# Casting loads on GpSimd's queue and crossbar transposes of q and k, in a kernel of sliding-window attention and a two-layer MLP

## Chip, core and metric

One core of a Trainium2 chip runs the kernel. The metric is the device time of one launch in microseconds (us). Five engines work side by side, each with a queue of its own: TensorE (PE; matmuls and transposes, its weight loads shown as PEld), VectorE (DVE), ScalarE (ACT), GpSimd (POOL) and SyncE (SP), which here only issues DMAs. DMAs are issued from a queue of an engine and carried out by sixteen DMA engines.

## The reference

```python
def _attn_ref(q, k, v):                      # each (8, 8, 576, 64), float32
    B, H, S, D = q.shape
    window = 128
    scores = np.matmul(q, k.transpose(0, 1, 3, 2)) / np.sqrt(D)
    rel = pos[:, None] - pos[None, :]
    slopes = 2.0 ** (-8.0 * (np.arange(H) + 1) / H)
    bias = slopes[:, None, None] * (-np.abs(rel))[None, :, :]
    mask = (rel >= 0) & (rel < window)
    scores = np.where(mask, scores + bias[None], -1e9)
    attn = softmax(scores)
    return np.matmul(attn, v)

def _moe_ref(x, w_in, w_out):                # x (4608, 512), w_in (512, 2048), w_out (2048, 512)
    h = x @ w_in
    g = h * np.clip(h + 3.0, 0.0, 6.0) / 6.0
    return g @ w_out
```

The attention output, with its heads side by side, is the `x` of the second part. A query sees itself and the 127 keys before it, so a block of 128 queries needs two blocks of 128 keys: its own (the diagonal block, lower triangle) and the one before (the off block, strictly upper triangle).

## The kernel before

**Attention.** The work goes by pair groups `g`: batch `b = g // 4` and a pair `hp = g % 4` of heads, 32 groups in all. A batch of 576 tokens is five blocks of tokens, the last of 64. For every group, `transposes` (L151) turns q and k by ten 128x128 TensorE transposes into `qT` and `kT`, through a PSUM tile `tp` that DVE copies out (L158). `scores_diag` (L161) multiplies the diagonal blocks of both heads into a PSUM tile `sc`, ACT takes the exponential (L173, with scale and position bias), and POOL cuts the triangle with an affine select (L176). `scores_off` (L181) does the same for the off blocks and for the last, 64-wide diagonal block (`p4`): L199, L202, and on POOL L204 and L207. `values` (L212) multiplies with v, to which a column of ones is appended, so that column 64 of `av` is the sum for the softmax; DVE takes its reciprocal (L230) and scales (L231). It is called twice, for blocks 0 to 2 and 3 to 4, with one `av` buffer. `back` (L235) transposes the result on TensorE and DVE copies it (L242) into `xT`, which keeps all 4,608 tokens.

**MLP.** It runs over nine tiles of 512 tokens in units of four matmuls of 512 columns. An up unit (`moe_up`, L248) makes one 128-row block of the hidden layer in a PSUM tile `hps` (two buffers); ACT makes a Relu of it (L257) and DVE the product (L258). A down unit (`moe_down`, L261) is a quarter of one 128-token output block; after the fourth, ACT or DVE copies the block to `osb` (L272, L274) and SP stores it (L275). A tile has 16 up and 16 down units; all are put in one list, and the down units of a tile go between the up units of the next. `fill(n)` (L286) puts the next n units of the list into TensorE's order, but an up unit only if the attention of every batch that its tokens come from is complete (`done`).

**Order.** The order of TensorE is written out by hand (L313 to L337): an iteration g does the scores of group g, the values and the back transposes of group g-1, the transposes of group g+1, and eight units of the list in between. The order on the other engines is left to the framework's scheduler. After the last iteration `fill` places what is left of the list.

**Loads.** q, k and v are loaded as float32 by SP's queue (`load_pair` for batch 0, `load_all`, L89, for the others: 15 DMAs per batch, each in pieces of 256 bytes, one head of one token) into four buffers, and cast to bfloat16: batch 0 by DVE (L132 to L137), the others by POOL (L142 to L147). Both weight matrices are loaded by POOL's queue, cast on the way, in four DMAs each (L119, L125).

PSUM has eight banks: `sc` two (one buffer), `av` one, `tp` two, `hps` two, `ops` (the down output) one.

Of the kernel before, what the change touches and what calls it, by code (L numbers as in the profile page):

```python
# [10 lines left out]
FP32 = mybir.dt.float32  # L11
# [7 lines left out]
def kernel(  # L19
# [20 lines left out]
    W = D + 1  # L40
    slopes = [2.0 ** (-8.0 * (h + 1) / H) for h in range(H)]
# [3 lines left out]
    n_nt = Ntok // NT  # L45

# [5 lines left out]
    bias3 = perm.tile([128, 1], FP32)  # L52
    rel_i = perm.tile([128, 1], INT32)
# [4 lines left out]
    loads = ctx.enter_context(tc.tile_pool(name="loads", bufs=4))  # L58
    held = ctx.enter_context(tc.tile_pool(name="held", bufs=1))
    qkt = ctx.enter_context(tc.tile_pool(name="qkt", bufs=3))  # L60
    ppool = ctx.enter_context(tc.tile_pool(name="ppool", bufs=3))
    small = ctx.enter_context(tc.tile_pool(name="small", bufs=4))
# [3 lines left out]
    ps_sc = ctx.enter_context(tc.tile_pool(name="ps_sc", bufs=1, space=bass.MemoryType.PSUM))  # L66
    ps_av = ctx.enter_context(tc.tile_pool(name="ps_av", bufs=1, space=bass.MemoryType.PSUM))
    ps_tp = ctx.enter_context(tc.tile_pool(name="ps_tp", bufs=2, space=bass.MemoryType.PSUM))
# [3 lines left out]
    qbuf = [held.tile([128, NQ, H * D], BF16, name=f"qbuf{i}") for i in range(2)]  # L72
    kbuf = [held.tile([128, NQ, H * D], BF16, name=f"kbuf{i}") for i in range(2)]
    vbuf = [held.tile([128, NQ, H, W], BF16, name=f"vbuf{i}") for i in range(2)]
    p4buf = [held.tile([128, 2, 128], BF16, name=f"p4buf{i}") for i in range(2)]

    srcs = (("qf", q), ("kf", k), ("vf", v))

    def new_loads():
        return {nm: loads.tile([128, NQ, H, D], FP32, tag="ld", name=nm) for nm, _ in srcs}  # L80

    def load_pair(got, b, hp):
        for nm, src in srcs:
            for h in (2 * hp, 2 * hp + 1):
                nc.sync.dma_start(out=got[nm][:, 0:4, h, :],
                                  in_=src[b, h, 0:512, :].rearrange("(t p) d -> p t d", p=128))
                nc.sync.dma_start(out=got[nm][:LAST, 4, h, :], in_=src[b, h, 512:S, :])  # L87

    def load_all(got, b):  # L89
        for nm, src in srcs:  # L90
            for j in range(NQ):
                n = min(128, S - j * 128)
                nc.sync.dma_start(
                    out=got[nm][:n, j, :, :],
                    in_=src[b, :, ds(j * 128, n), :].rearrange("h p d -> p h d"))

    got0 = new_loads()
    for hp in range(NP):
        load_pair(got0, 0, hp)

    make_identity(nc, ident)
    nc.vector.memset(bias3, 0.5)
    nc.gpsimd.iota(rel_i, pattern=[[0, 1]], base=0, channel_multiplier=1)
    nc.vector.tensor_copy(out=rel_f, in_=rel_i)
    for h in range(H):
        nc.vector.tensor_scalar(out=bias_d[:, h:h + 1], in0=rel_f, scalar1=-64.0,
                                scalar2=slopes[h], op0=ALU.add, op1=ALU.mult)
        nc.vector.tensor_scalar(out=bias_o[:, h:h + 1], in0=rel_f, scalar1=-192.0,
                                scalar2=slopes[h], op0=ALU.add, op1=ALU.mult)
    for i in range(2):  # L110
        nc.vector.memset(vbuf[i][:, :, :, D:W], 1.0)
        nc.vector.memset(vbuf[i][64:128, 4, :, 0:D], 0.0)
        nc.vector.memset(qbuf[i][64:128, 4, :], 0.0)
        nc.vector.memset(kbuf[i][64:128, 4, :], 0.0)
        nc.vector.memset(p4buf[i], 1.0)
# [13 lines left out]
    def cast_pair(got, b, hp, eng):  # L129
        for nm, dst in (("qf", qbuf[b % 2]), ("kf", kbuf[b % 2])):  # L130
            s = got[nm].rearrange("p j h d -> p j (h d)")
            eng.tensor_copy(out=dst[:, 0:4, ts(hp, 128)], in_=s[:, 0:4, ts(hp, 128)])  # L132
            eng.tensor_copy(out=dst[:LAST, 4, ts(hp, 128)], in_=s[:LAST, 4, ts(hp, 128)])
        hs = slice(2 * hp, 2 * hp + 2)
        vb = vbuf[b % 2]
        eng.tensor_copy(out=vb[:, 0:4, hs, 0:D], in_=got["vf"][:, 0:4, hs, :])
        eng.tensor_copy(out=vb[:LAST, 4, hs, 0:D], in_=got["vf"][:LAST, 4, hs, :])  # L137

    def cast_all(got, b):
        for nm, dst in (("qf", qbuf[b % 2]), ("kf", kbuf[b % 2])):  # L140
            s = got[nm].rearrange("p j h d -> p j (h d)")
            nc.gpsimd.tensor_copy(out=dst[:, 0:4, :], in_=s[:, 0:4, :])  # L142
            nc.gpsimd.tensor_copy(out=dst[:LAST, 4, :], in_=s[:LAST, 4, :])
        vb = vbuf[b % 2]
        nc.gpsimd.tensor_copy(out=vb[:, 0:4, :, 0:D].rearrange("p j h d -> p (j h) d"),
                              in_=got["vf"][:, 0:4, :, :].rearrange("p j h d -> p (j h) d"))
        nc.gpsimd.tensor_copy(out=vb[:LAST, 4, :, 0:D], in_=got["vf"][:LAST, 4, :, :])  # L147

    st = {}

    def transposes(g):  # L151
        b, hp = divmod(g, NP)
        for src, nm in ((qbuf[b % 2], "qT"), (kbuf[b % 2], "kT")):
            tp = ps_tp.tile([128, SP], BF16, tag="tp", name="tp")
            for j in range(NQ):
                nc.tensor.transpose(tp[:, ts(j, 128)], src[:, j, ts(hp, 128)], ident)  # L156
            t = qkt.tile([128, SP], BF16, tag=nm, name=nm)
            nc.vector.tensor_copy(out=t, in_=tp)  # L158
            st[g, nm] = t

    def scores_diag(g):  # L161
        b, hp = divmod(g, NP)
        qT, kT = st[g, "qT"], st[g, "kT"]
        sc = ps_sc.tile([128, 2, 512], FP32, tag="sc", name="sc")
        for j in range(4):
            for e in range(2):
                r = slice(e * D, (e + 1) * D)
                nc.tensor.matmul(sc[:, e, ts(j, 128)], lhsT=kT[r, ts(j, 128)],  # L168
                                 rhs=qT[r, ts(j, 128)], start=True, stop=True)
        pd = ppool.tile([128, 2, 4, 128], BF16, tag="pd", name="pd")  # L170
        for e in range(2):
            h = 2 * hp + e
            nc.scalar.activation(out=pd[:, e, :, :].rearrange("p j c -> p (j c)"),  # L173
                                 in_=sc[:, e, :], func=ACT.Exp,
                                 bias=bias_d[:, h:h + 1], scale=scale)
            nc.gpsimd.affine_select(out=pd[:, e, :, :], in_=pd[:, e, :, :],  # L176
                                    pattern=[[0, 4], [1, 128]], channel_multiplier=-1, base=0,
                                    compare_op=ALU.is_ge, fill=0.0)
        st[g, "pd"] = pd

    def scores_off(g):  # L181
        b, hp = divmod(g, NP)
        qT, kT = st[g, "qT"], st[g, "kT"]
        sc = ps_sc.tile([128, 2, 512], FP32, tag="sc", name="sc")
        for j in range(4):
            n = 128 if j < 3 else LAST
            for e in range(2):
                r = slice(e * D, (e + 1) * D)
                nc.tensor.matmul(sc[:, e, ds(j * 128, n)], lhsT=kT[r, ts(j, 128)],  # L189
                                 rhs=qT[r, ds((j + 1) * 128, n)], start=True, stop=True)  # L190
        for e in range(2):
            r = slice(e * D, (e + 1) * D)
            nc.tensor.matmul(sc[:, e, 448:512], lhsT=kT[r, 512:640],  # L193
                             rhs=qT[r, 512:576], start=True, stop=True)
        po = ppool.tile([128, 2, 4, 128], BF16, tag="po", name="po")
        p4 = p4buf[g % 2]
        for e in range(2):
            h = 2 * hp + e
            nc.scalar.activation(out=po[:, e, :, :].rearrange("p j c -> p (j c)"),  # L199
                                 in_=sc[:, e, :], func=ACT.Exp,  # L200
                                 bias=bias_o[:, h:h + 1], scale=scale)
            nc.scalar.activation(out=p4[:, e, 0:64], in_=sc[:, e, 448:512], func=ACT.Exp,  # L202
                                 bias=bias_d[:, h:h + 1], scale=scale)
            nc.gpsimd.affine_select(out=po[:, e, :, :], in_=po[:, e, :, :],  # L204
                                    pattern=[[0, 4], [-1, 128]], channel_multiplier=1, base=-1,
                                    compare_op=ALU.is_ge, fill=0.0)
        nc.gpsimd.affine_select(out=p4[:, :, 0:64], in_=p4[:, :, 0:64],  # L207
                                pattern=[[0, 2], [1, 64]], channel_multiplier=-1, base=0,
                                compare_op=ALU.is_ge, fill=0.0)
        st[g, "po"] = po  # L210
# [157 lines left out]
```

The softmax here doesn't subtract the row's maximum and nothing guards it: scores larger than these inputs give would overflow.

## Time and profile before

| | |
|---|---|
| median of three runs | 419.68 us (418.04 to 422.31) |
| time of the profiled execution | 419.74 us |
| its span, first to last instruction | 417.7 us |
| TensorE busy | 338.9 us (81%) |
| VectorE busy | 201.5 us (48%) |
| ScalarE busy | 198.5 us (48%) |
| GpSimd busy | 145.1 us (35%) |
| granted TensorE clock, mean | 0.996 |
| read from HBM / written | 36.70 MB / 9.44 MB |

A profile line of the timeline has the start in us, the duration, the engine, the line of the kernel, the operation, output and input tile, shapes, how many instructions are merged (x4), and in brackets how long the engine stood idle before it and what released it. Busy time of TensorE is a modelled quantity and can be high while matmuls are spaced out. The numbers of the page's slices are tenths of busy time, 9 for 90% or more.

### The profile page before, as it was taken

The numbers are of one execution on the slowest core, as the hardware profiler recorded it, in microseconds if no ns is written. First come the engines' busy times: TensorE is split into PE (matmuls) and PEld (weight loads), VectorE is DVE, ScalarE is ACT, GpSimd is POOL, SyncE is SP. The second block draws the span as 40 slices with busy tenths as digits, with TensorE's granted clock in tenths as the row PEclk, the third lists the DMA queues.
The fourth block names the chain that finished last, engine by engine and source line by source line (L and its number), as shares of the span: only waits on it lengthen the run. The fifth ranks groups of instructions, "written<-read, shape, count | busy, mean of one in ns | idle before, by whom it ended". The sixth has DMA issues, their size and how long they took to land.

```text
span 417.7 us, 7115 instructions
## 1 busy us (share of the span) xinstructions
PE 338.9 (81%) x2739; PEld 175.2 (42%) x2784; DVE 201.5 (48%) x438; ACT 198.5 (48%) x355; POOL 145.1 (35%) x217
## 2 busy tenths in 40 slices
PE   0141618878999899989998999899899999999985
PEld 0021415445444444444454444444444444444432
DVE  3341614675455555555555555555555454344400
ACT  0240414675655565555565655556565534443400
POOL 3070464458657427342752374222222200000000
PEclk9999999998999999999999999999999999999999
DMA  8989799997157989898470000001000000101011
GB/s 134 195 148 199 151 198 197 209 201 135 49 132 166 179 176 166 161 186 152 116 163 25 27 26 27 27 27 39 32 31 27 27 25 30 48 25 52 25 70 55
DMA packets 122481, 42.40 MB, mean 101 GB/s; under 512 B 113744, under 2 KB 117840, under 8 KB 122448
## 3 DMA queue, kind: packets, MB, share of 16 engines
q1 hardware_dynamic: 118224, 37.76, 44.3%
q0 software_dynamic: 4224, 4.19, 6.2%
q8 instruction: 21, 0.34, 0.4%
q14 instruction: 12, 0.10, 0.1%
HBM read 36.70 MB, written 9.44 MB: 110 GB/s over the span
## 4 chain that ended last, share of the span: by engine, by line
PE 46%; DVE 15%; ACT 14%; issue 11%; DMA 8%; SPq 4%; POOL 1%; DVEq 0%; POOLq 0%; ACTq 0%
PE ops L267 22%; PE hps L253 13%; ACT r L257 8%; DMA vf<-in_v_dram 6%; DVE g L258 5%; DVE avs L231 4%; DVE osb L274 3%; ACT pd L173 3%; PE tp L156 2%; PE sc L168 2%; PE av L222 2%; PE sc L189 2%; ACT p4buf L202 2%; SPq L87 2%; DMA kf<-in_k_dram 2%
## 5 line engine op out<-in xcount | busy, mean ns | idle before, releaser
L258 DVE SCALAR_TENSOR_TENSOR g<-r,hps 128x512 bf16<-128x512 f32 x144 | 99.0, 687 | 117.0 <-ACT r L257 116.9
L253 PE MATMUL hps<-xT,w_in_sb 128*128 128x512 bf16 x535 | 144.4, 382 | 10.5 <-DVE xT L242 5.3
L267 PE MATMUL ops<-w_out_sb,g 128*128 128x512 bf16 x572 | 145.2, 379 | 5.6 <-DVE osb L274 3.1
L257 ACT ACTIVATE r<-hps,bias 128x512 f32<-128x512 f32 x144 | 99.2, 691 | 96.8 <-PE hps L253 93.9
L267 PEld LDWEIGHTS <-g 128*128 128x128 bf16 x576 | 53.6, 98 | 70.0 <-issue 15.1
L176 POOL TENSOR_SCALAR_AFFINE_SELECT pd<-pd 128x512 bf16<-128x512 bf16 x64 | 39.8, 644 | 96.9 <-ACT pd L173 96.9
L253 PEld LDWEIGHTS <-w_in_sb 128*128 128x128 bf16 x576 | 49.8, 98 | 49.9 <-issue 4.1
L204 POOL TENSOR_SCALAR_AFFINE_SELECT po<-po 128x512 bf16<-128x512 bf16 x64 | 40.4, 634 | 79.0 <-ACT po L199 75.7
L199 ACT ACTIVATE po<-sc,bias_o 128x512 bf16<-128x512 f32 x64 | 44.0, 687 | 39.3 <-PE sc L193 39.3
L173 ACT ACTIVATE pd<-sc,bias_d 128x512 bf16<-128x512 f32 x64 | 40.5, 683 | 43.1 <-PE sc L168 43.1
L222 PE MATMUL av<-vbuf,po 128*128 128x65 bf16 x256 | 26.1, 201 | 15.4 <-DVE avs L231 15.3
L158 DVE COPY qT<-tp 128x640 bf16<-128x640 bf16 x32 | 15.7, 492 | 35.9 <-PE tp L156 35.8
L156 PE MATMUL tp<-ident,kbuf 128*128 128x128 bf16 x160 | 16.4, 239 | 20.0 <-DVE kbuf L132 15.9
L231 DVE TENSOR_TENSOR avs<-av,rc 128x384 bf16<-128x384 f32 x64 | 31.4, 491 | 2.0
L156 PE MATMUL tp<-ident,qbuf 128*128 128x128 bf16 x160 | 16.2, 238 | 19.5 <-DVE qbuf L132 15.2
L222 PEld LDWEIGHTS <-po 128*128 128x128 bf16 x256 | 18.9, 102 | 29.3 <-DVE avs L231 29.0
L225 PE MATMUL av<-vbuf,pd 128*128 128x65 bf16 x256 | 25.0, 201 | 0.0
L156 PEld LDWEIGHTS <-qbuf 128*128 128x128 bf16 x160 | 12.1, 105 | 26.2 <-DVE qbuf L132 15.5
L225 PEld LDWEIGHTS <-pd 128*128 128x128 bf16 x256 | 20.0, 101 | 7.2 <-issue 0.8
L156 PEld LDWEIGHTS <-kbuf 128*128 128x128 bf16 x160 | 11.4, 106 | 21.6 <-DVE kbuf L132 16.9
L202 ACT ACTIVATE p4buf<-sc,bias_d 128x64 bf16<-128x64 f32 x64 | 20.2, 315 | 0.0
L274 DVE COPY osb<-ops 128x512 f32<-128x512 f32 x18 | 12.3, 685 | 16.0 <-PE ops L267 16.0
(46 smaller groups left out, 231.8 us busy)
## 6 DMA issues: line engine op xcount, KB each, us to landing
out_dram<-osb SPq DMA_DIRECT2D x36, 256.0 KB, 2.0
qf<-in_q_dram SPq DMA_DIRECT2D x28, 256.0 KB, 4.9
kf<-in_k_dram SPq DMA_DIRECT2D x28, 256.0 KB, 5.1
vf<-in_v_dram SPq DMA_DIRECT2D x28, 256.0 KB, 4.9
w_in_sb<-in_moe_w_in_dram POOLq DMA_DIRECT2D x4, 512.0 KB, 10.4
w_out_sb<-in_moe_w_out_dram POOLq DMA_DIRECT2D x4, 512.0 KB, 10.1
qf<-in_q_dram SPq DMA_DIRECT2D x15, 128.0 KB, 5.3
kf<-in_k_dram SPq DMA_DIRECT2D x15, 128.0 KB, 4.8
```

Of the source, the lines that this page charges most:

```text
L156: nc.tensor.transpose(tp[:, ts(j, 128)], src[:, j, ts(hp, 128)], ident)
L173: nc.scalar.activation(out=pd[:, e, :, :].rearrange("p j c -> p (j c)"), in_=sc[:, e, :], func=ACT.Exp, bias=bias_d[:, h:h + 1], scale=scale)
L176: nc.gpsimd.affine_select(out=pd[:, e, :, :], in_=pd[:, e, :, :], pattern=[[0, 4], [1, 128]], channel_multiplier=-1, base=0, compare_op=AL ...
L199: nc.scalar.activation(out=po[:, e, :, :].rearrange("p j c -> p (j c)"), in_=sc[:, e, :], func=ACT.Exp, bias=bias_o[:, h:h + 1], scale=scale)
L204: nc.gpsimd.affine_select(out=po[:, e, :, :], in_=po[:, e, :, :], pattern=[[0, 4], [-1, 128]], channel_multiplier=1, base=-1, compare_op=A ...
L222: nc.tensor.matmul(av[:, i, e, :], lhsT=po[:, e, qt - 1, :], rhs=vb[:, qt - 1, h, :], start=True, stop=False)
L225: nc.tensor.matmul(av[:, i, e, :], lhsT=d, rhs=vb[:, qt, h, :], start=(qt == 0), stop=True)
L231: nc.vector.tensor_tensor(out=st[g, "avs"][:, qts[0]:qts[0] + nq, :, :], in0=av[:, 0:nq, :, 0:D], in1=rc[:, 0:nq, :, :].to_broadcast([128, ...
L253: nc.tensor.matmul(hps, lhsT=w_in_sb[:, ks, ts(ms, 128)], rhs=xT[:, ks, ts(nt, NT)], start=(ks == 0), stop=(ks == n_ks - 1))
L257: nc.scalar.activation(out=r6, in_=hps, func=ACT.Relu, bias=bias3[:, 0:1], scale=1.0 / 6.0)
L258: nc.vector.scalar_tensor_tensor(out=gts[nt][:, ms, :], in0=r6, scalar=1.0, in1=hps, op0=ALU.min, op1=ALU.mult)
L267: nc.tensor.matmul(ops[nt, sub], lhsT=gts[nt][:, ms, ts(sub, 128)], rhs=w_out_sb[:, ms, :], start=(ms == 0), stop=(ms == n_ms - 1))
```

## The change

- **Loads.** The float32 buffers and every cast instruction go. All of q, k and v is loaded by GpSimd's queue with a cast on the way, straight into bfloat16 buffers. For batches 0 and 1, q and k are loaded as runs: 96 partitions with six consecutive tokens each, 1,536 contiguous bytes per head (`load_runs`). v, and q and k of batches 2 to 7, are loaded by token in pieces of 256 bytes, five DMAs per tensor and batch (`load_tokens`). v has three buffers. `stage_next(g)` issues the loads of later batches and of the weights at the end of each iteration.
- **Transposes of q and k.** Batches 0 and 1: `prepare` copies a pair's runs together on DVE, then twelve TensorE transposes of 96 rows; DVE copies q out, ACT copies k. Batches 2 to 7: SP issues ten DMA transposes per batch (`xbar`) from the token buffers into `qTb` and `kTb`, which hold a whole batch, twice. `XBAR_X` is False, so x is still transposed on TensorE.
- **Scores.** Diagonal and off blocks are computed together (`scores`), into two `sc` buffers. The exponentials are placed one by one between the units.
- **Masks.** The off masks are a multiplication with a 0/1 tile on DVE (`cut_off`); the other two masks stay on POOL.
- **PSUM.** `sc` takes four banks; `tp` and the tile of the back transposes now come from the two `hps` buffers.
- **Units.** Batch 0 has no units between its groups, eight follow it, batch 1 has two per group, the later groups eight. The list of the first two tiles is rearranged. In the last tile two output blocks use `hps` buffers, and the last block is copied and stored in two halves.
- **Order.** The order of all five engines is now the written one.
- The exponential's table is loaded by a first small activation (`warm`).

```diff
+    def load_runs(b, hs):
+        for nm, src in (("q", q), ("k", k)):
+            nc.gpsimd.dma_start(out=runs(b, nm)[:, hs, :],
+                                in_=src[b, hs, :, :].rearrange("h (p t) d -> p h (t d)", t=RT))
+
+    def load_tokens(b, nm, src):
+        for j in range(NQ):
+            n = min(128, S - j * 128)
+            o = (vbuf[b % 3][:n, j, :, 0:D] if nm == "v" else
+                 tokens(b, nm)[:n, j, :].rearrange("p (h d) -> p h d", h=H))
+            nc.gpsimd.dma_start(
+                out=o, in_=src[b, :, ds(j * 128, n), :].rearrange("h p d -> p h d"))
...
+    def xbar(b, nm, j):
+        n = min(128, S - j * 128)
+        dst = (qTb if nm == "q" else kTb)[b % 2]
+        nc.sync.dma_start_transpose(out=dst[:, :, ds(j * 128, n)], in_=tokens(b, nm)[:n, j, :])
...
+    def cut_off(g, e):
+        po = st[g, "po"][:, e, :, :]
+        nc.vector.tensor_tensor(out=po, in0=po, in1=mask_off.to_broadcast([128, 4, 128]),
+                                op=ALU.mult)
...
+    xb = [(nm, j) for nm in "qk" for j in range(NQ)]
+
+    def stage_next(g):
+        b, hp = divmod(g, NP)
+        if g == 1:
+            load_weights_in()
+        if g == 2:
+            load_runs(1, slice(0, H))
+        if g == 3:
+            load_tokens(1, "v", v)
+        if g == NP:
+            load_weights_out()
+        nm, nb, src = {0: ("k", b + 1, k), 1: ("v", b + 1, v), 3: ("q", b + 2, q)}.get(
+            hp, (None, 0, None))
+        if g == NP:
+            load_tokens(2, "q", q)
+        if (g > 2 * NP or hp == 3) and NB_PE < nb < B or g == 2 * NP:
+            load_tokens(nb, nm, src)
+        if g == NP + 1:
+            load_tokens(2, "k", k)
+        if g == NP + 2:
+            load_tokens(2, "v", v)
+        if b + 1 >= NB_PE and b + 1 < B:
+            for nm, j in ((), xb[0:4], xb[4:8], xb[8:10])[hp]:
+                xbar(b + 1, nm, j)
+
+    def segment(lo, hi, fills):
+        for g in range(lo, hi + 1):
+            f = fills(g)
...
+            if g + 1 < hi and (g + 1) // NP < NB_PE:
+                transposes(g + 1)
+            if g < hi:
+                scores(g)
+            fill(f[0])
+            if g < hi:
+                exp_diag(g, 0)
+            fill(f[1])
+            if g < hi:
+                exp_diag(g, 1)
+            if g > lo:
+                values(g - 1, (0, 1, 2))
+            fill(f[2])
+            if g < hi:
+                exp_off(g, 0)
+            fill(f[3])
+            if g < hi:
+                exp_off(g, 1)
+            if g > lo:
+                values(g - 1, (3, 4))
+            if g + 2 < hi and (g + 2) // NP < NB_PE:
+                prepare(g + 2)
+            if g < hi:
+                cut_off(g, 0)
+            fill(f[4])
+            if g < hi:
+                cut_off(g, 1)
+            if g > lo:
+                back(g - 1)
...
+            fill(f[5])
+            if g < hi:
+                stage_next(g)
+            fill(f[6])
...
+        segment(0, NP, lambda g: (0,) * 7)
+        fill(8)
+        prepare(NP)
+        transposes(NP)
+        prepare(NP + 1)
+        segment(NP, G, lambda g: (0, 0, 0, 1, 0, 0, 1) if g < 2 * NP else (1, 1, 1, 1, 1, 1, 2))
+        done[0] = G
         fill(len(units))
```

## The prediction

> **What bounds the kernel now.** First the profile's page, its forty slices and its queues.
>
> ```profile
> PE   0141618878999899989998999899899999999985
> DMA  8989799997157989898470000001000000101011
> q1 hardware_dynamic: 118224, 37.76, 44.3%
> q0 software_dynamic: 4224, 4.19, 6.2%
> ```
>
> A slice is 10.4 us. DMA is full and TensorE mostly empty in the first six slices, TensorE full from the tenth on. So there is a start that waits for data and a long stage that TensorE sets. Then the timeline, the first exponential (ACT) of pair groups 8, 9 and 31:
>
> ```profile
> 97.51 1.26 ACT L173 ACTIVATE pd<-sc,bias_d 128x512 bf16<-128x512 f32 x2 [0.79 <-PE sc L168]
> 103.64 1.27 ACT L173 ACTIVATE pd<-sc,bias_d 128x512 bf16<-128x512 f32 x2 [0.51 <-PE sc L168]
> 323.18 1.26 ACT L173 ACTIVATE pd<-sc,bias_d 128x512 bf16<-128x512 f32 x2 [0.80 <-PE sc L168]
> ```
>
> Columns: start, duration, engine. Batch 2 begins at 97.5; from group 9 to 31 an iteration takes (323.18-103.64)/22 = 9.98 us. One iteration, timeline from 183 us:
>
> ```profile
> 185.50 1.03 PE L253 MATMUL hps<-xT,w_in_sb 128*128 128x512 bf16 x4
> 186.57 0.69 ACT L257 ACTIVATE r<-hps,bias 128x512 f32<-128x512 f32 x1 [1.16 <-PE hps L253]
> 186.89 0.20 PE L222 MATMUL av<-vbuf,po 128*128 128x65 bf16 x1 [0.36 <-DVE avs L231]
> 187.29 0.69 DVE L258 SCALAR_TENSOR_TENSOR g<-r,hps 128x512 bf16<-128x512 f32 x1 [0.46 <-ACT r L257]
> 187.90 0.17 DVE L230 RECIPROCAL rc<-av 128x4 f32<-128x4 f32 x1
> 188.11 0.42 DVE L231 TENSOR_TENSOR avs<-av,rc 128x256 bf16<-128x256 f32 x1
> ```
>
> An up unit starts, 1.07 later its Relu, 0.72 later its product, 0.61 later the next DVE operation, 0.21 later the scaling that the values wait for. TensorE itself loses little here (0.36 at 186.89, waiting for `av`). Last, the DMA view of 0 to 20 us and of 100 to 240 us (packets, MB, share of 16 engines), and POOL's issue of the weights:
>
> ```profile
> q0 software_dynamic: 2112, 2.10, 65.3%
> ```
> ```profile
> q1 hardware_dynamic: 58676, 17.70, 62.9%
> ```
> ```profile
> 1.56 3.11 POOL L119 DMA_DIRECT2D w_in_sb<-in_moe_w_in_dram  x4
> ```
>
> Packet prices: 0.629x140x16/58,676 = 24 ns for a 256 B piece on SP's queue; 0.653x20x16/2,112 = 99 ns for a casting 2 KB piece on POOL's. POOL spends 0.78 us per DMA of 512 pieces.
>
> **Steady stage.** Removed per iteration from batch 2 on: ten transposes (189.31 to 189.87: 0.56 us of PE), two DVE copies (0.49+0.48), two POOL selects (2x0.63), POOL's casts (52 us in all). Added on DVE: two masks of 128x512, each between 0.41 (cast of that size, L136) and 0.69 (L258); I take 0.5, nearest to the all-SBUF cast. They pay for the copies that go.
>
> All queues now run in written order, so I walk one iteration. TensorE: both score blocks 0.66, down 0.86, up 0.86, first values 0.30, down 0.86, up: this up starts at 3.54. The second values, their reciprocal and scaling stand behind that up's product on DVE: 1.07+0.72+0.61+0.21+0.47 (scaling to next matmul) = 3.08, so the back transposes start at 6.62 and not at 5.5. They take 0.28, then up, down, up 2.59: 9.49, with 0.1 of issue gaps 9.6. ACT (4x0.58 Relu, 4x0.58+2x0.20 Exp) fits inside it. Against 9.98: -0.38 x 22 = -8. Behind the scaling DVE still has mask, output copy 0.68, mask and the xT copy 0.45, ending at 8.2 to 8.7; the last up needs the shared ps_h buffer at 8.65. That cover is gone if masks get slower. Rows show that POOL slows DVE: a 64x128 cast (L133) takes 0.21 alone, and
>
> ```profile
> 22.77 0.76 POOL L125 DMA_DIRECT2D w_out_sb<-in_moe_w_out_dram  x1
> 23.02 0.66 DVE L133 CAST kbuf<-kf 64x128 bf16<-64x128 f32 x1
> ```
>
> 0.66 beside a DMA issue. Two masks at +0.45 with 0 to 0.45 of cover: up to 0.5 per iteration, 11 us; I take 0 and keep 11 for the range. [...]
>
> **Transposes on SP.** 60 transposes of up to 128x512; none in this trace. Queue ahead of them: the output stores, in order. In the last iteration of a batch the store goes at about 7.2 (its ACT copy ends then), then k's last two transposes, and the next batch's scores wait at 9.6. Issue: 0.36 each (store, L275) to 1.3 (crowded load, L93). Landing: 2.0 (store) to 5.8 (load). So k lands at 9.9 to 15.6: 0.3 to 6 us late, times 5 boundaries. SBUF to SBUF without HBM is nearer to the short row: 1.5 x5 = +7.5, range 1.5 to 30. In DMA time one costs 0.3 us (64 pieces of 2 KB at a store's 77 ns) to 0.77 (512 pieces of 256 B at 24): I take 0.77, because a transposed row is 256 B; 7.7 per batch. [...]
>
> **Loads.** Per later batch 13,824 pieces of 256 B. On POOL's queue with a cast they aren't in the trace: below 24 ns by a little (they write half), above 99 (eight times the bytes); I take 24, because the read, 256 B from HBM, is the same. 20.7 us, stores 2.8, transposes 7.7: 31.2 of 39.9 (four iterations and 1.5): 8.7 spare. POOL pays 0.78 to 1.56 (twice the pieces) per DMA, 15 per batch: 12 to 23 us beside 6 of selects; it fits, and a burst of 8 us delays only masks needed an iteration later. SP loses its loads.
>
> **Start.** q and k of batches 0 and 1 come as 1,536 pieces of 1.5 KB per batch, 24 to 99 ns, linear 70: 6.7 us; v 6.9; each weight matrix 13. Heads 4-5 stand behind v: data at about 16 (2 first byte, 1.7+1.7+6.9+1.7 moving, 2 landing). So group 1's scores at 18, then 6 us per iteration (before: 19.47 to 25.26 between exponentials), last back transposes at 37, eight up units at 1.26 (83.73-81.21 for two) to 47, batch 1 at 50 with 6 us each: compute is ready for group 8 at 74. DMA: w_in is issued by POOL after group 1's masks, 23, lands 37; q,k of batch 1 44; v 51; w_out is issued after group 4's masks, 54, lands 67; q(2) 74, k(2) 81, transposes 85. So DMA sets it: group 8 at 85 against 97.1: -12. Bounds: 75 (compute alone) and 97 (POOL late by two bursts): -22 to 0.
>
> **Tail.** The last tile's four output groups used one PSUM bank: idle 0.67, 0.78 and 0.72 before three of them.
>
> ```profile
> 401.51 3.61 PE L267 MATMUL ops<-w_out_sb,g 128*128 128x512 bf16 x15 [0.67 <-ACT osb L272]
> ```
>
> ps_h takes two of them: -2.2, and the halved last copy -0.3. The table load (1.28 at 17.1) moves into waiting for data; the other constants and the mask build lie there too, as the memsets do now (DVE idle until 8.5).
>
> **Sum.** Against the profiled execution, 419.74 us (span 417.7 and 2.0 around it; the median is 419.68): -12 -8.4 +7.5 -2.5 = 404.3. Its own range: 388 to 415.
>
> **Rivals.** *Small casting pieces are slow* (slower): each ns above 24 delays the start by 18,432/16 = 1.15 us; beyond 34 ns (8.7/0.864) every later batch is DMA-bound and adds 0.864x5 more. At 34: 416; it decides from 34.6 ns, only 1.4 times the row; 40 ns gives 449, 50 gives 504. For: 99 ns for a casting piece is the only row of its queue. Against: eight times the data. *Transposes land late* (slower): 6 us at each boundary is 22.5 more: 427. *Queue order eats the gain*: masks and xT late by 0.5, 404+11 = 415, with a small further delay no change. *Nothing waits*: group 8 at 75 and no boundary stall: 387. That loads aren't cast on the way can't be: no other cast is left.
>
> **How the numbers follow.** This kernel's repeats lie 1% apart (418.04 to 422.31), so less can't be told from no change. Forecast 0.45, nothing waits 0.10, no change 0.10, slow pieces 0.20, late transposes 0.15: faster 0.55, same 0.10, slower 0.35. Range 385 to 455 reaches through late transposes and slow pieces to 41 ns; it leaves out the slower half of those (0.10) and a little below.
>
> **What would show it.** Group 8's first exponential near 85; spacing 9.6 from group 9 on, longer by 1 to 2 where a batch starts, with scores waiting for kTb; POOL's queue at 24 ns per piece and DMA under 0.85 in the steady slices; tail without its three gaps. Wrong if DMA stays at 9 until the last batch, if TensorE waits for qTb by more than 3 us per batch, or if "av" and "hps" wait longer for DVE than now.

## Result and profile after

| | before | after |
|---|---|---|
| median | 420.44 us (418.04 to 422.31) | 431.56 us (430.88 to 432.37) |
| ratio, with its 95% interval | | 1.0268 (1.0209 to 1.0328) |
| span of the profiled execution | 417.7 us | 429.0 us |
| its granted TensorE clock, mean | 0.996 | 0.936 |
| TensorE busy | 338.9 us | 339.9 us |

The change is slower by 2.7%; the forecast was 404 us, faster. The page of the changed kernel, its slices (10.7 us each) and queues:

```profile
PE   3468755258984999589958995899889989999986
PEclk9999678659996899899999999899999999999999
DMA  9699089999949987969893999199200001010112
...
q0 software_dynamic: 101216, 18.36, 56.3%
q1 hardware_dynamic: 34752, 16.39, 18.3%
```

TensorE is busy from the first slices on, so the start did get shorter. But its row now has a 4 or 5 in every fourth slice (12, 16, 20, 24, counted from 0), where the row of before is all 8 and 9, and the granted clock dips too. The first exponentials of groups 8, 9 and 31 (timeline):

```profile
88.75 1.26 ACT L197 ACTIVATE pd<-scd,bias_d 128x512 bf16<-128x512 f32 x2 [9.06 <-PE scd L177]
100.08 0.68 ACT L197 ACTIVATE pd<-scd,bias_d 128x512 bf16<-128x512 f32 x1
337.91 0.68 ACT L197 ACTIVATE pd<-scd,bias_d 128x512 bf16<-128x512 f32 x1
```

From them, stage by stage:

| stage | before | after | difference |
|---|---|---|---|
| to group 8 | 97.51 | 88.75 | -8.8 |
| group 8 to 9 | 6.13 | 11.33 | +5.2 |
| group 9 to 31 | 219.54 | 237.83 | +18.3 |
| group 31 to the end of the span | 94.5 | 91.0 | -3.5 |

In the third row most iterations take 9.35 us (9.98 before), which would be 205.7 for 22. The other 32 us lie at the first two iterations of each batch. The spacing of exponentials there, after minus 9.35, for batches 3 to 7: 9.3+1.1, 2.3+3.9, 2.4+4.3, 2.5+4.3, 0+1.8, together 31.9 (group 10 has the rest). The waits name what is late (`scd` and `sco` are the PSUM tiles of the diagonal and of the off scores):

```profile
PE scd L177 <- DMA kTb<-kbuf: 20.4, 8, 5.1
...
PE sco L188 <- DMA kTb<-kbuf: 6.7, 6, 1.5
...
POOL kbuf L100 <- DMA w_out_sb<-in_moe_w_out_dram: 4.7, 3, 1.7
```

Columns: us in total, times, longest. Both score matmuls wait for the transposed k: 27.1 us, 9.2 of them at group 8 and 17.9 at the later batches. The place itself, the timeline where batch 4 begins (group 16):

```profile
172.72 0.33 SPq L304 DMA_DIRECT2D out_dram<-osb  x1
172.75 4.22 POOL L100 DMA_DIRECT2D qbuf<-in_q_dram  x5 [0.21 <-issue]
...
173.15 2.54 SPq L141 DMA_TRANSPOSE kTb<-kbuf  x2
...
175.48 0.34 PE L177 MATMUL scd<-qTb,kTb 64*128 64x128 bf16 x6
...
178.18 0.23 PE L177 MATMUL scd<-qTb,kTb 64*128 64x128 bf16 x2 [2.36 <-DMA kTb<-kbuf]
...
179.96 0.24 PE L188 MATMUL sco<-qTb,kTb 64*128 64x64 bf16 x2 [1.35 <-DMA kTb<-kbuf]
180.53 1.48 PE L289 MATMUL ops<-w_out_sb,g 128*128 128x512 bf16 x3 [0.33 <-issue]
```

The first six of eight score matmuls run, the last two wait for the last two transposes of k, issued at 173.15. At the same moment, from 172.75, POOL issues the five loads of q of batch 5. The kernel has its own control: at group 28 the order on SP is the same, but no batch is left to load.

```profile
304.62 0.33 SPq L304 DMA_DIRECT2D out_dram<-osb  x1
...
305.04 2.52 SPq L141 DMA_TRANSPOSE kTb<-kbuf  x2
...
307.38 0.40 PE L177 MATMUL scd<-qTb,kTb 64*128 64x128 bf16 x8
...
308.74 0.20 PE L188 MATMUL sco<-qTb,kTb 64*128 64x64 bf16 x2 [0.77 <-DMA kTb<-kbuf]
309.10 0.81 PE L289 MATMUL ops<-w_out_sb,g 128*128 128x512 bf16 x3 [0.16 <-issue]
```

The same two transposes take 2.52 us to issue, yet no diagonal block waits and the whole loss is 0.77. The DMA issues of these places give 5.2 us to landing at group 16 and 2.4 at group 28. There is a second difference: three output matmuls take 1.48 us after the wait of group 16 and 0.81 at group 28. The windows 174 to 178 and 178 to 186 us (after the length: PE, PEld, DVE, ACT, POOL busy, then granted clock, DMA share, GB/s) show why. The DMA share adds up the times of packets, which overlap, so it can exceed 1.

```profile
174.00:178.00 4.00, 1.82 (x14) 0.66 (x11) 1.38 (x2) 1.23 (x2) 2.97 (x4) 1.00 1.42 136
178.00:186.00 8.00, 5.96 (x47) 2.87 (x49) 1.35 (x3) 3.35 (x7) 1.26 (x2) 0.79 0.69 43
```

In the slow stretch matmuls of 512 columns start 0.43 us apart (1.48 us for three), elsewhere 0.22. Within the second window the clock is 1.00 up to 179 us and from 183 on, and 0.50 from 180 to 182.5. At those two values, 0.79 over 8 us is (1-0.79)x8x2 = 3.4 us at half speed. So a late transpose is paid for twice: by the wait, and by slow matmuls behind it.

### The profile page after: what moved, and what is told of

Read it like the earlier page. It is cut to its first block, busy times and chain, and to the rows that moved or that the text cites. A ratio compares the mean times of both kernels' runs of the same rounds, so it can differ in the third digit from the quotient of the medians.

```text
span 429.0 us, 6639 instructions
## 1 busy us (share of the span) xinstructions
PE 339.9 (79%) x2516; PEld 168.6 (39%) x2560; DVE 198.7 (46%) x440; ACT 203.4 (47%) x365; POOL 148.6 (35%) x222
## 3 DMA queue, kind: packets, MB, share of 16 engines
q1 hardware_dynamic: 34752, 16.39, 18.3%
## 4 chain that ended last, share of the span: by engine, by line
PE 50%; ACT 15%; DVE 13%; DMA 9%; issue 7%; SPq 3%; POOL 2%; DVEq 0%; ACTq 0%; POOLq 0%
PE hps L272 22%; PE ops L289 19%; DMA kTb<-kbuf 8%; ACT r L276 5%; DVE g L277 5%; ACT pd L197 4%; ACT po L207 4%; DVE avs L241 3%; SPq L141 3%; PE scd L177 2%; DVE osb L303 2%; DVE po L219 1%; ACT p4buf L210 1%; PE tb L262 1%; PE sco L184 1%
## 5 line engine op out<-in xcount | busy, mean ns | idle before, releaser
L272 PE MATMUL hps<-xT,w_in_sb 128*128 128x512 bf16 x566 | 155.4, 397 | 7.7 <-DVE xT L263 3.6
L197 ACT ACTIVATE pd<-scd,bias_d 128x512 bf16<-128x512 f32 x64 | 42.6, 682 | 17.5 <-PE scd L177 17.5
L207 ACT ACTIVATE po<-sco,bias_o 128x512 bf16<-128x512 f32 x64 | 44.0, 687 | 0.0
L262 PE MATMUL tb<-ident,avs 128*128 128x128 bf16 x160 | 21.2, 236 | 17.3 <-DVE avs L241 17.0
L100 POOL DMA_DIRECT2D vbuf<-in_v_dram x40 | 33.8, 868 | 0.9 <-issue 0.9
L232 PE MATMUL av<-vbuf,po 128*128 128x65 bf16 x256 | 27.1, 205 | 8.4 <-DVE avs L241 8.1
L177 PE MATMUL scd<-qTb,kTb 64*128 64x128 bf16 x256 | 15.5, 237 | 20.4 <-DMA kTb<-kbuf 20.4
L240 DVE RECIPROCAL rc<-av 128x6 f32<-128x6 f32 x64 | 11.8, 184 | 38.5 <-PE av L235 38.5
L100 POOL DMA_DIRECT2D kbuf<-in_k_dram x30 | 25.3, 864 | 6.1 <-DMA w_out_sb<-in_moe_w_out_dram 4.7
L219 DVE TENSOR_TENSOR po<-po,mask_off 128x512 bf16<-128x512 bf16 x64 | 26.4, 437 | 0.0
L100 POOL DMA_DIRECT2D qbuf<-in_q_dram x30 | 25.4, 872 | 0.9 <-issue 0.9
```

The lines of the kernel that those rows point to most:

```text
L100: nc.gpsimd.dma_start(out=o, in_=src[b, :, ds(j * 128, n), :].rearrange("h p d -> p h d"))
L219: nc.vector.tensor_tensor(out=po, in0=po, in1=mask_off.to_broadcast([128, 4, 128]), op=ALU.mult)
L232: nc.tensor.matmul(av[:, i, e, :], lhsT=po[:, e, qt - 1, :], rhs=vb[:, qt - 1, h, 0:W], start=True, stop=False)
L272: nc.tensor.matmul(hps, lhsT=w_in_sb[:, ks, ts(ms, 128)], rhs=xT[:, ks, ts(nt, NT)], start=(ks == 0), stop=(ks == n_ks - 1))
```

## Experiments

Theory 1: the loads of q issued in the same moment share the DMA engines with the last transposes and delay their landing. Theory 2: those transposes are late by themselves, being issued last on SP behind a store. Theory 3: the small casting pieces fill the DMA engines, so that all is late whatever the order. Beside these, how much is the clock's, and what the start and the masks cost. All ratios are to the kernel before, run on the same chip; it took 421.36 us beside x1 to x4, 419.53 beside x5 to x7 and 419.55 beside x8 and x9, so a difference between medians of two of these sets can be off by 1 to 2 us.

| run | edit | median us | ratio (95% interval) |
|---|---|---|---|
| x1_q_early | q loads one iteration earlier | 409.44 | 0.9749 (0.9693 to 0.9805) |
| x2_x_early | transposes one iteration earlier | 403.80 | 0.9606 (0.9557 to 0.9655) |
| x4_dummy | filler matmuls in the wait | 425.93 | 1.0146 (1.0082 to 1.0211) |
| x3_no_xbar | all transposes on TensorE | 447.90 | 1.0644 (1.0581 to 1.0707) |
| x5b_order_only | w_out's load behind batch 2's | 420.58 | 1.0026 (1.0002 to 1.0051) |
| x5_w_out_late | the same on top of x2 | 391.71 | 0.9339 (0.9302 to 0.9376) |
| x6_mask_pool | x2, off masks on POOL | 398.63 | 0.9497 (0.9463 to 0.9531) |
| x7_down_first | x5, down unit first in the list | 386.44 | 0.9211 (0.9182 to 0.9240) |
| x8_late_mask_pool | x5 and x6 together | 385.20 | 0.9182 (0.9133 to 0.9232) |
| x9_all | x8 and x7 together | 383.09 | 0.9121 (0.9062 to 0.9179) |

**Only the competing loads moved.** From batch 2 on the q loads of a batch are issued at the end of its third iteration instead of its fourth. The transposes stay where they are.

```diff
-        nm, nb, src = {0: ("k", b + 1, k), 1: ("v", b + 1, v), 3: ("q", b + 2, q)}.get(
-            hp, (None, 0, None))
+        nm, nb, src = {0: ("k", b + 1, k), 1: ("v", b + 1, v),
+                       2 if b > 1 else 3: ("q", b + 2, q)}.get(hp, (None, 0, None))
...
-        if (g > 2 * NP or hp == 3) and NB_PE < nb < B or g == 2 * NP:
+        if (g > 2 * NP or g == 2 * NP - 1) and NB_PE < nb < B or g == 2 * NP:
```

> From batch 2 on the loads of q(b+2) are issued one iteration earlier (second to last of a batch), nothing else. Theory 1: at a batch's end the last two k transposes share the DMA engines with the five q loads that POOL issues at the same moment, land 5 to 8 us after issue and not 2 to 3, and TensorE waits in the next batch's scores and then runs at half clock. Where no load runs beside them (group 28) the wait is 0.8 us. So groups 12, 16, 20 and 24 become like 28 (extra of two iterations 1.8 us in place of 10.4, 6.3, 6.7, 6.8): -23 us, about 409. Theory 2 (SP's order: store and issue of 1.2 us each are what is late): within 3 us of 431. Theory 3 (pieces at 32 ns make the steady stage DMA-bound): within 3 us of 431, with the waits moved to other groups.

409.44: 22 us less than the changed kernel. The excess at the batch starts falls from 32 to 11 us, and plain iterations stay at 9.35. Timeline of the same place as above (group 16):

```profile
165.38 0.33 SPq L304 DMA_DIRECT2D out_dram<-osb  x1
165.80 2.52 SPq L141 DMA_TRANSPOSE kTb<-kbuf  x2
168.14 0.64 PE L177 MATMUL scd<-qTb,kTb 64*128 64x128 bf16 x6
...
169.65 0.23 PE L177 MATMUL scd<-qTb,kTb 64*128 64x128 bf16 x2 [0.87 <-DMA kTb<-kbuf]
```

SP's queue is the same as before the edit: store, then two transposes, issued in 2.52 us. With no loads issued beside them (the last of the earlier ones are still moving) the two transposes land in 3.2 us instead of 5.2, the diagonal block waits 0.87 instead of 2.36, and `sco` not at all. From group 12 on the waits for `kTb` fall from 17.9 us to 4.6, and the granted clock over 100 to 320 us rises from 0.95 to 1.00. This shows theory 1 for most of the loss, and speaks against theory 3: over 100 to 300 us as many casting pieces move, with packet times as long as before (33.6 ns, 32.6 in the changed kernel), and the kernel is 22 us faster. Whether the transposes are held up on the DMA engines themselves or on the way to and from them was not taken apart.

**Transposes moved, loads left.** The groups of transposes go one iteration forward, so that the last two have a whole iteration to land.

```diff
-            for nm, j in ((), xb[0:4], xb[4:8], xb[8:10])[hp]:
+            for nm, j in (xb[0:4], xb[4:8], xb[8:10], ())[hp]:
```

> All crossbar transposes one iteration earlier (4, 4 and 2 in the first, second and third iteration of a batch), loads as in the changed kernel. Theory 1: no wait for kTb from group 12 on, about 408. Theory 2: the same 408, since the store ahead of them no longer counts. Theory 3: 425 to 432, waits for q or k tokens in place of those for kTb. Together with the run that moves q's loads it tells 1 from 2.

403.80, below the 408 that theories 1 and 2 both expected. The waits of its whole trace for `kTb`:

```profile
PE scd L177 <- DMA kTb<-kbuf: 8.1, 4, 4.7
PE sco L188 <- DMA kTb<-kbuf: 0.6, 1, 0.6
```

All five are at group 8. From batch 3 on nothing waits for `kTb` any more, although the transposes' median landing is longer (6.3 us, 5.4 in the changed kernel), and the clock over 100 to 320 us is 1.00. Groups 9 to 31 take 210.8 us instead of 237.8. The excess at the batch starts, 11 us in x1, is 4.8. What x1 still lost by its late issue, 5.6 us of the median, is theory 2's share. Theory 3 falls: from group 13 on iterations keep 9.35 us except where a batch begins, and no wait of TensorE moves to another transfer. (The DMA share over 100 to 300 us is 0.94; since it can exceed 1, it doesn't tell how much room is left.)

**The clock alone.** Sixteen matmuls of 512 columns stand ahead of the scores where batches 3 to 6 begin, so that TensorE works while it would wait. This adds work, and nothing reads the result.

```diff
+        if hp == 0 and 3 * NP <= g < 7 * NP:
+            dm = ps_h.tile([128, 512], FP32, tag="h", name="dm")
+            for _ in range(16):
+                nc.tensor.matmul(dm, lhsT=w_in_sb[:, 0, 0:128], rhs=xT[:, 0, 0:512],
+                                 start=True, stop=True)
```

> The changed kernel with sixteen extra 512-column matmuls (3.5 us, result unused) ahead of the scores of groups 12, 16, 20 and 24, where TensorE waits for kTb. Theory 1 with the clock: the units after the wait take 0.86 and not 1.3 to 1.9 us, about 1 us less at each of three groups and 3 at group 12: 425 or somewhat less, mean clock above 0.95. If the clock plays no part in the loss: 431 to 436.

425.93, 5.6 us faster with more work. Group 16 in its timeline:

```profile
173.59 3.62 PE L175 MATMUL dm<-xT,w_in_sb 128*128 128x512 bf16 x16
177.14 0.40 PE L182 MATMUL scd<-qTb,kTb 64*128 64x128 bf16 x8
...
178.31 0.20 PE L193 MATMUL sco<-qTb,kTb 64*128 64x64 bf16 x2 [0.58 <-DMA kTb<-kbuf]
178.45 1.04 PE L294 MATMUL ops<-w_out_sb,g 128*128 128x512 bf16 x4
```

and the window behind the wait:

```profile
178.00:186.00 8.00, 6.39 (x47) 3.11 (x49) 4.18 (x10) 3.82 (x8) 3.05 (x5) 1.00 0.16 11
```

The clock there is 1.00 and not 0.79. The fill covers nearly all of the wait, and four output matmuls behind it take 1.04 us, where three took 1.48 without it. The spacing to group 16 is longer (12.6 instead of 11.7), that to group 17 shorter (11.2 instead of 13.2). Between groups 9 and 31 the run takes 233.6 us instead of 237.8, so the half clock cost at least these 4.2 us; the rest of the 5.1 between the two profiled executions lies ahead of group 9, where the edit changes nothing. Its whole share is larger: the four fills take 4x3.6 = 14.5 us and remove 11.2 us of waiting for `kTb` (17.9 to 6.7), so without a gain behind the waits the run would have lost 3.3; that makes 7.5. Another way: of the 32 us, 17.9 are waits and 4.8 remain in x2, which leaves 9 or so for what follows a wait.

**No crossbar at all.** q and k of every batch are loaded as runs and transposed on TensorE, as batches 0 and 1 are (`NB_PE = B`; `stage_next` loads runs and v of batch b+1).

> q and k of every batch as runs of 1.5 KB and transposed on TensorE, no crossbar transpose; the rest of the changed kernel. Per iteration twelve transposes more on TensorE (0.67 us), one more copy each on DVE and ACT (0.75, 0.64) and two pair copies on DVE: 9.35 becomes 10.0 to 10.4, without the batch ends: 22 iterations 220 to 229 in place of 238; batch 2 ready up to 8 us earlier. All theories: 405 to 422. If it beats the runs with early transposes, the crossbar itself is the loss; if not, only its timing.

447.90, far outside. The waits give the reason:

```profile
PE tp L162 <- DVE g L277: 28.8, 24, 1.2
```

The transposes' PSUM tile `tp` shares two buffers with the up units, so each of 24 groups waits 1.2 us for the product on DVE; with 0.84 us for its twelve transposes an iteration takes 11.3 us and more. The run says that in this kernel, with this PSUM, the crossbar pays. It doesn't say what TensorE transposes would cost with a bank of their own, as the kernel before had; that wasn't tried.

**The start.** In the changed kernel w_out is issued ahead of q and k of batch 2. POOL's and SP's timeline there:

```profile
53.80 3.02 POOL L134 DMA_DIRECT2D w_out_sb<-in_moe_w_out_dram  x4
56.78 4.31 POOL L100 DMA_DIRECT2D qbuf<-in_q_dram  x5
64.44 0.90 POOL L100 DMA_DIRECT2D kbuf<-in_k_dram  x1 [1.61 <-DMA w_out_sb<-in_moe_w_out_dram]
...
76.72 7.22 SPq L141 DMA_TRANSPOSE kTb<-kbuf  x5
...
88.36 0.29 PE L177 MATMUL scd<-qTb,kTb 64*128 64x128 bf16 x2 [1.34 <-DMA kTb<-kbuf]
```

POOL even waits for parts of w_out to land before it can issue k. The edit issues q(2) behind v(1), then k(2) and v(2), and w_out last. Once alone, once on top of x2:

```diff
         if g == 3:
             load_tokens(1, "v", v)
+            load_tokens(2, "q", q)
         if g == NP:
+            load_tokens(2, "k", k)
+            load_tokens(2, "v", v)
+        if g == NP + 1:
             load_weights_out()
...
-        if g == NP:
-            load_tokens(2, "q", q)
...
-        if g == NP + 1:
-            load_tokens(2, "k", k)
-        if g == NP + 2:
-            load_tokens(2, "v", v)
```

> The same order of loads with the crossbar transposes left where the change put them. If the start and the batch ends are separate losses, it gains the same 15 us on the changed kernel, 416 (412 to 420), and the waits at groups 12, 16, 20 and 24 stay. If the one makes room for the other, much more or much less.

420.58, just outside its range: group 8 comes at 76.8 and group 9 12.8 us earlier, but from there to group 31 it takes 240.8 instead of 237.8. The waits for `kTb` from group 12 on are the same (18.1 us, 17.9 in the changed kernel), but the clock over 100 to 320 us is 0.93 and not 0.95, so more of the work behind them runs slowly. Why the same waits cost more clock here is open.

> The early transposes, and the loads of q, k and v of batch 2 put ahead of those of w_out (q behind v of batch 1, k and v in iteration 4, w_out in iteration 5). Theory of the start: group 8 waits for its k transposes because 13 us of w_out stand ahead of q and k on the DMA engines; compute alone would be there at 77 (70.8 for group 7 and 6.3 more) instead of 88; and without the wait the next iteration is 7 to 8 us and not 11.4, since TensorE keeps its clock. 403.8-11-4 = 389, range 386 to 394. If instead POOL's bursts or compute set group 8: 400 to 404.

391.71, 12.1 us below x2. Its two first exponentials of groups 7 and 8:

```profile
70.74 1.26 ACT L197 ACTIVATE pd<-scd,bias_d 128x512 bf16<-128x512 f32 x2
...
77.43 1.26 ACT L197 ACTIVATE pd<-scd,bias_d 128x512 bf16<-128x512 f32 x2
```

No wait in brackets, and TensorE waits for no DMA anywhere in this trace: compute alone sets group 8 at 77.4, 10.9 us earlier, as expected. But group 8 to 9 takes 10.0 instead of 11.4 us and not the 7 to 8 expected; the clock is still 0.80 there (77.4 to 87.4 us).

**The masks.** In x2 the batch starts still lose 0.85 us each. Its timeline where batch 4 begins:

```profile
172.57 0.41 DVE L219 TENSOR_TENSOR po<-po,mask_off 128x512 bf16<-128x512 bf16 x1
...
173.50 0.42 DVE L219 TENSOR_TENSOR po<-po,mask_off 128x512 bf16<-128x512 bf16 x1
173.84 0.45 DVE L263 COPY xT<-tb 128x576 bf16<-128x576 bf16 x1
174.34 0.38 PE L272 MATMUL hps<-xT,w_in_sb 128*128 128x512 bf16 x1 [0.70 <-DVE xT L263]
```

Where a batch ends, the next up unit reads the tokens that have just been copied into `xT`, and on DVE both masks stand ahead of that copy. x6 makes the cut on POOL again, by an affine select directly behind the exponential, and drops `cut_off`:

```diff
+        nc.gpsimd.affine_select(out=po[:, e, :, :], in_=po[:, e, :, :],
+                                pattern=[[0, 4], [-1, 128]], channel_multiplier=1, base=-1,
+                                compare_op=ALU.is_ge, fill=0.0)
...
-        nc.vector.tensor_tensor(out=po, in0=po, in1=mask_off.to_broadcast([128, 4, 128]),
-                                op=ALU.mult)
+        pass
```

> The early transposes, with the off masks back as affine selects on POOL (64 times 0.63 us there, 64 times 0.44 less on DVE). If the masks on DVE are hidden, as the prediction took them: iteration 9.35 and total 403 to 405. If they hold up the copy of xT or the scaling, up to 0.5 per iteration less: 393. If POOL's descriptor bursts then delay the selects: some groups wait for POOL, 405 to 415.

398.63, 5.2 us below x2 (4.7 between the profiled executions), and between the cases expected. The copy at the same place now starts at

```profile
171.28 0.45 DVE L264 COPY xT<-tb 128x576 bf16<-128x576 bf16 x1
```

in an iteration whose first exponential comes at 164.8 instead of 166.9, so 0.5 us earlier within it, and the extra time of a batch start falls from 0.85 to 0.2. The rest, some 1.5 us, comes from the start; plain iterations are 9.35 in both.

**Combinations.** x7 puts the down unit ahead of the up unit in the list of every tile from the third on, on top of x5:

```diff
+            units.append((nt, moe_down, step))
...
-            units.append((nt, moe_down, step))
```

> As the run with w_out late, with the down unit ahead of the up unit in the list from the third tile on, so that at a batch's end the first unit behind the back transposes doesn't read the xT that they are still copying (0.7 to 0.85 us at each of six batch ends). The chain of Relu, product, scaling then starts from another unit: iteration between 9.2 and 9.7. 389 less 5 if the iteration stays 9.35, 389 to 393 if it grows by 0.2 to 0.4.

386.44, 5.3 us below x5: iterations alternate between 9.6 and 9.1, and a batch start no longer waits for `xT`, since the up unit comes later. From group 13 to 29, four whole batches, x5 takes 153.0 us and x7 149.5.

> Early transposes, w_out late, off masks on POOL. The three gains are at three places (batch ends, start, the copy of xT at batch ends): 391.7 less the 5.2 that the masks on POOL gained = 386.5, range 384 to 389. If POOL, with descriptors of 0.85 us each ahead of the selects, is late: 390 or more.

385.20, 6.5 below x5. The same four batches take 150.4 us.

> The same with the down unit first. Down first (5.3 us with masks on DVE) and masks on POOL both shorten the wait of a batch's first up unit for xT, 0.7 to 0.85 us at each of six ends, so they don't add up: 385 to 387, 1 to 2 below the better of the two alone. If they add up: 381.

383.09, below the 385 to 387 expected, but only 2.1 below x8. The four batches take 149.3 us: of 153.0, down first alone saves 3.5, the masks on POOL alone 2.6, both 3.7. Each of the two edits removes the wait for `xT` by itself, so the gains do not add. What x9 gains beyond that lies outside these batches and was not taken apart. This is the best version, 0.9121 of the kernel before.

## Why the prediction was wrong

**The step that failed** is the one on the transposes: "1.5 x5 = +7.5, range 1.5 to 30". The batch starts lost 32 us; 27 of them (237.8 less 210.8 between groups 9 and 31) went when the transposes were issued early (x2), so that is what the term should have been, and 4.8 stayed, mostly a wait for `xT` that the sum put at nothing. The mechanism was named as a rival (transposes land late, 427) and given 0.15; in the sum its price was taken from the wrong row. That the rival's 30 us lie near 27 is partly luck: it priced a wait of 6 us per boundary, but the waits come to 17.9 us in all, and what is missing is the clock. I took the landing of a store (2.0 us) because an SBUF to SBUF transfer "is nearer to the short row". The runs show that what counts is what else is issued at that moment: 2.4 us to landing without loads (group 28), 5.2 beside five of them (group 16). The edit's own text had the loads of q at the same `hp == 3` as the last transposes, and my budget of DMA time ("8.7 spare" per batch) spread that load evenly over four iterations, where it comes in bursts. x1 agrees: with those loads alone issued elsewhere the two transposes land in 3.2 us.

**A price left out altogether** is the clock. I charged a wait with its length. At group 16 TensorE ran at half speed for about 3.4 us behind it (a clock of 0.79 over 178 to 186 us); at group 12, with waits of 4.50 and 1.09 us, the clock was 0.50 from 132 to 141. Taken at clocks of 1.00 and 0.50 alone, as read at these two groups, means of 0.936 and 0.996 make, as an estimate, (1-0.936)x429.0x2 = 55 us at half speed against 3 before. Only some 20 of them lie between 100 and 320 us (a clock of 0.95); most of the rest lie in the start (0.83, 0.75 and 0.57 in the three stretches of 20 us from 40 to 100), where TensorE waits for data anyway. At group 16 waits of 2.36 and 1.35 us with a few matmuls between them were enough; how short a wait still leaves the clock at 1.00 was not tested.

**Casting pieces** were priced at 24 ns, as uncast ones. While nothing but v's loads moves (DMA view, 104 to 116 us; packets, MB, share):

```profile
q0 software_dynamic: 4688, 0.59, 77.2%
```

0.772x12x16/4,688 = 31.6 ns of packet time. That is short of the 34.6 from which that rival would have decided, and x1 and x2 show that it did not. But packet time, in which all these prices are counted, is not the time that a DMA engine is taken up. The same view in two busy stretches of 2 us, casting pieces in the changed kernel (110 to 112) and uncast ones in the kernel before (154 to 156):

```profile
q0 software_dynamic: 2142, 0.27, 211.5%
```
```profile
q1 hardware_dynamic: 2036, 0.51, 129.1%
```

Shares above 100% say that packets overlap, and both kinds move at about the same pace, one piece per engine in 15 and 16 ns. So a longer packet time doesn't mean a lower rate, and the prediction's DMA budgets ("31.2 of 39.9") were no measure of how full the engines are. A transposed piece of 256 B was taken at 24 ns. In the changed kernel from 100 to 300 us SP's queue moved 23,136 packets in 24.6% of the engines' time; less 18 stores of 128 packets at 77 ns, (787-177)/20,832 = 29 ns of packet time remain, somewhat more. SP takes 1.2 us (median) to issue each of a batch's ten transposes, 12 us per batch.

**The start** was sized nearly right and for the right reason: batch 1 predicted at 50, measured 49.2; group 8 at 85, DMA-set, measured 88.75; the compute bound 74, measured 77.4 in x5. Two small slips of the working do not change that: the line between 24 and 99 ns gives 78 ns for a run of 1.5 KB and not 70, and against the 97.51 of its own row, 85 is -12.5. What I missed came behind it: TensorE waits at group 8 for the transposes of batch 2, 9.2 us in all, the next iteration runs on a slow TensorE (a clock of 0.57 from 80 to 100 us) and takes 11.3 instead of 6.1. That gave 5.2 of the 8.8 back. Not all of it is the clock's: in x8, with a clock of 1.00 and no wait for `kTb`, the same iteration still takes 8.6.

**The steady iteration** was right in kind and sized too small: walked at 9.6, measured 9.35, so 13.8 us off 22 iterations and not 8.4. Which term of the walk was too long was not taken apart. Masks were taken at 0.5 and took 0.44. That a DMA issue of POOL delays a DVE operation by 0.45, as a row of before had it (0.66 us against 0.21), was rarely so (median of the masks 0.416, maximum 0.853). But their cover was costed in the wrong place: I had them hidden until the last up unit needs a PSUM buffer at 8.65; where a batch ends the first up unit needs `xT` itself, and there they showed, about 5 us in all with the start (x6). POOL's issue, 0.87 us per DMA (mean; most have 1,024 pieces), lay near the low end of 0.78 to 1.56.

**The tail** was right: -3.5 for -2.5, and the last tile's output is one block of 63 matmuls without the three gaps.

```profile
411.01 13.97 PE L289 MATMUL ops<-w_out_sb,g 128*128 128x512 bf16 x63 [1.24 <-DVE osb L303]
```

Put together from the stages: 419.74 - 8.8 + 5.2 - 13.8 + 32.1 - 3.5 = 430.9, for a profiled execution of 430.88. That the stages add up is no proof; what each is due to rests on the runs above.

## What to carry to other kernels

Price a transfer by what else is issued at that moment on any queue, not by its landing alone (two transposes of SP's landed in 5.2 us beside five loads of POOL's, in 3.2 with those issued earlier), and check DMA time by bursts and not by batch; a share that can exceed 1 (211.5% in a stretch above) doesn't tell what room is left. Where a transfer's consumer sits on the bounding engine, issue it a whole stage ahead: one reordered tuple was worth 28 us here. Charge a TensorE wait with the slow matmuls behind it too (1.48 us for three behind the wait of group 16, 0.81 at group 28), and when a step is called hidden, look for the iteration in which its cover is absent.

## What was not expected of the hardware

- TensorE at half clock for about 3.4 us (0.79 over 178 to 186 us, 0.50 from 180 to 182.5) after waits of 2.36 and 1.35 us at group 16; filler matmuls in the wait made groups 9 to 31 4.2 us faster (x4).
- A packet of a casting load of 256 B pieces takes 31.6 ns, one without a cast on SP's queue took 24 in the kernel before; yet both move at one piece per engine in 15 to 16 ns where the queue is busy, since packets overlap.
- POOL waited three times, 4.7 us in all, for parts of w_out to land before it issued k, with four DMAs of w_out and five of q issued ahead. Which limit that is wasn't tried.
- A transpose of up to 128x512 takes SP 1.2 us to issue (median), against 0.33 for a store.
